# A second level of products in the second layer, shared by pairs of batches

## The chip, the cores and the metric

The kernel runs on one core of a Trainium2 chip. The metric is the device time of one execution in microseconds. The engines are named as in the profile: PE (matmuls), PEld (its weight loads), DVE (vector), ACT (scalar), POOL (GpSimd) and SP, whose queue issues nearly all DMAs.

## The reference

The input has 8 batches of 12 heads, 448 tokens and 64 columns per head, in float32. Attention with normalised q and k gives a row of 768 numbers per token, and two layers without biases follow:

```python
q_n, k_n = rmsnorm(q, g_q), rmsnorm(k, g_k)
scores = matmul(q_n, k_n.transpose(0, 1, 3, 2)) / sqrt(64)
attn = exp(scores - max) / (sum + 1e-9)
x = matmul(attn, v)              # heads side by side: (8*448, 768)
h = x @ w_in                     # w_in: (768, 2048)
out = (h - tanh(h)) @ w_out      # w_out: (2048, 768)
```

The output has 3584 rows (8 batches of 448) and 768 columns. The weights arrive as float64 and are rounded to float32 in the kernel.

## The kernel before

The order of the work on every engine is written out by hand. There are two streams. The attention stream goes through 48 steps, six per batch; a step treats two heads, and steps with `s >= 2 * NP` (12 and later) are made by `slot(s)`. The MLP stream is the generator `mlp()`, which yields after each matmul. `slot` begins with a visit (values of head pair `s` and scores of `s + 1`, on PE, then `divide`), and then has 14 points; before each, `run(...)` lets the MLP stream issue matmuls for a share of the step, and at the point a piece of attention's other work is issued: squares, sums of squares and a power on POOL (`power_blocks`, L488), `scale_blocks` (L495), transposes (L505, L509), sums of the probabilities (`add` L562, `add_third` L568, `add_last` L575), and their folding (L672 to L704). `gap_ns(s)` says how much MLP work goes into a step, and the MLP stream runs about one batch behind attention: steps 12 and later carry batches 1 to 6, and batch 7's two layers come after the last step.

Both layers use a Strassen product in the form with seven products and shared sums. The first layer (`hidden(b)`) splits the 768 columns in two halves, the 2048 in two halves, and the batch's 448 tokens in two halves of 224. It has four sets (`SETS`) of seven products, each of 2 x 3 matmuls of 128 x 128 weights with 224 moving columns. The sums of the tokens' quarters are made in `divide`, on POOL (L733 to L736), into the tile `tt`. The activations `h - tanh(h)` go into `gT` by `shrink` (L811, L812). The second layer (`project(b)`) has three sets of seven products, each of 8 matmuls of 224 columns; the sums of `gT` that it needs are made in `factors` and `rest` (L822 to L824 on DVE and POOL, L856 on POOL) into the tile `tg`. Finished output rows are transposed on DVE by `store` (L870) into one of two `th` buffers, and four DMAs (L875) per buffer write them out two products later.

The products are issued in the order `ORDER = (1, 5, 6, 2, 3, 7, 4)`. Products 2, 3 and 7 accumulate into the PSUM banks of 1, 5 and 6. There are three such banks, `mm0` to `mm2`, in turn. After each product DVE or ACT reads the bank (`use`). Work that can wait by one product is put into `late["todo"]`.

The seven combinations of each layer's weights are made once, in batch 0, and stored in DRAM (`w_in_dram`, `w_out_dram`). From batch 1 on a ring of six SBUF slots is filled from there by SP, in the order of `ring_steps`; `ring_load` is called four products ahead (L397, L399).

Of the kernel before, what the change touches and what calls it, by code (L numbers as in the profile page):

```python
# [20 lines left out]
NCH = 4  # L21
# [123 lines left out]
def bounded_path(tc, ctx, q, k, v, moe_w_in, moe_w_out, out, g_col, ident, ones, half_ones, neg_half, early):  # L145
# [32 lines left out]
    SETS = CF // 4  # L178
    ORDER = (1, 5, 6, 2, 3, 7, 4)
# [18 lines left out]
    gp = pool("gp", bufs=1)  # L198
    wp_stack = ctx.enter_context(ExitStack())
# [14 lines left out]

    def load(s, names):
        b, hp = steps[s]
        for name in names:
            src = {"q": q, "k": k, "v": v}[name]
            if s == 0 and name != "v":
                t = early[name]  # L220
            else:
                shape = [CP, 2, NCH, D] if name == "q" else [P, NCH, 2, D] if name == "k" else [P, 2, NCH, D]
                t = nat.tile(shape, F32, name=f"{name}_nat", bufs=3 if name == "v" else 2)
                fetch(nc, name, t, src[b, 2 * hp : 2 * hp + 2], in_order(s))
# [9 lines left out]
    BLOCKS = {1: 0, 2: 1, 4: 2, 7: 3, 5: 4, 6: 5, 3: 6}  # L234
    w_out_dram = scratch.tile([P, 7, HC, HF, P], F32, name="w_out")
# [140 lines left out]
    def ring_slot():  # L376
# [4 lines left out]
    ring_steps = [  # L381
        (b, layer, j, p)
        for b in range(1, B)
        for layer, count in ((0, SETS), (1, HC))
        for j in range(count)
        for p in ORDER
    ]
    ring_tiles = {}

    def ring_load(to):  # L390

        for n in range(len(ring_tiles), min(to, len(ring_steps))):
            b, layer, j, p = ring_steps[n]
            t = ring_tiles[ring_steps[n]] = ring_slot()
            if layer == 0:
                assert kept[1] > j
                nc.sync.dma_start(out=t[:, : 2 * HALF], in_=w_in_dram[j, p])  # L397
            else:
# [55 lines left out]
    def load_blocks(s):  # L454
        b, hp = steps[s]
        t = loaded["qk", s] = late["blocks"].tile([P, 2, NJ, BL], F32, name="qk_nat", bufs=2)
# [249 lines left out]
    def divide(s, av):  # L706
        b, hp = steps[s]
        rs = whole.pop(s)
        x = xT[b, hp] = xp.tile([P, S], F32, name="xT")
# [15 lines left out]
        if hp < HC:  # L725
            return
        c = hp - HC
        if c == 0:
            tt[b] = tp.tile([P, 3, HC, HS], F32, name="tt", bufs=1)
        eng = nc.vector if b == 0 and c == HC - 1 else nc.gpsimd  # L730
        x11, x12, x21, x22 = (xT[b, r][:, n : n + HS] for r in (c, hp) for n in (0, HS))
        t1, t2, t4 = (tt[b][:, i, c] for i in range(3))
        eng.tensor_tensor(out=t1, in0=x12, in1=x11, op=ALU.subtract)  # L733
        eng.tensor_tensor(out=t2, in0=x22, in1=t1, op=ALU.subtract)  # L734
        eng.tensor_tensor(out=x12, in0=x22, in1=x12, op=ALU.subtract)
        eng.tensor_tensor(out=t4, in0=x21, in1=t2, op=ALU.subtract)  # L736
# [16 lines left out]
    def products(b, layer, count, width, depth, moving, done_with):  # L753
# [8 lines left out]
        def product(j, p, bank, first):  # L762
# [21 lines left out]
            for fn in now:  # L784
                fn()

# [9 lines left out]
    def hidden(b):  # L796

        g = late["g"] = gp.tile([P, CF, S], F32, name="gT")
# [676 lines left out]
```

## Time and profile before

| | |
|---|---|
| Median of 3 runs | 1382.25 us (1381.95 to 1382.39) |
| Profiled execution | 1382.1 us, span 1380.2 us |
| Mean granted PE clock | 0.995 |
| PE busy | 1347.5 us (98%) |
| PEld busy | 1127.5 us (82%) |
| DVE busy | 891.1 us (65%) |
| ACT busy | 551.7 us (40%) |
| POOL busy | 553.7 us (40%) |
| DMA, mean | 181 GB/s |

Busy times are sums over one profiled execution. PE's matmuls overlap, so PE's busy time says that it was occupied, not that it ran at its peak. One matmul of the program leaves two records in the trace. The first 286 us hold batch 0, whose weights are still being made; after them the steps repeat, and the last 148.5 us of PE's work hold MLP matmuls alone.

### The profile page before, as it was taken

The page shows a single profiled execution, that of the slowest core. Times are in us where ns is not written, and L with a number is a line of the kernel's source. Part 1 is how long each engine was busy: PE and PEld are TensorE (multiplying, and loading weights), DVE is VectorE, ACT ScalarE, POOL GpSimd, SP SyncE. Part 2 cuts the span into 40 slices and gives each one's busy share as a digit, 9 for nine tenths or more (in the row PEclk, how much of TensorE's full clock was granted, in tenths as well). Part 3 has the DMA queues.
Part 4 walks back from the last instruction along what each step waited for, and adds up shares of the span by engine and source line. Part 5 has one row for each costly group of instructions (what it writes and reads, how often), then busy time and mean ns, then how long its engine had stood idle before and what let it go on. Part 6 is the DMA issues. An engine that isn't in the chain of part 4 may idle for free.

```text
span 1380.2 us, 29907 instructions
## 1 busy us (share of the span) xinstructions
PE 1347.5 (98%) x11840; PEld 1127.5 (82%) x11840; DVE 891.1 (65%) x1378; ACT 551.7 (40%) x1314; POOL 553.7 (40%) x345
## 2 busy tenths in 40 slices
PE   7989899999999999999999999999999999999997
PEld 3467654478998998899899889989988998999997
DVE  4999889856854776567765568547765677533311
ACT  7856555244433443334433344334433344211100
POOL 4656566224632356215542346323563155302300
PEclk9999999999999999999999999999999999999999
DMA  7789788965676567567657656765665665556664
GB/s 169 180 226 238 242 255 225 256 166 145 184 199 160 153 189 195 155 145 203 186 147 200 169 147 190 197 156 154 192 190 157 155 196 168 141 162 183 192 187 90
DMA packets 367656, 249.90 MB, mean 181 GB/s; under 512 B 281748, under 2 KB 309780, under 8 KB 367508
## 3 DMA queue, kind: packets, MB, share of 16 engines
q1 hardware_dynamic: 367504, 247.90, 66.7%
q8 instruction: 96, 1.57, 0.5%
q14 instruction: 52, 0.43, 0.1%
q10 hardware_dynamic: 4, 0.00, 0.0%
HBM read 214.40 MB, written 33.42 MB: 180 GB/s over the span
## 4 chain that ended last, share of the span: by engine, by line
PE 89%; DVE 5%; DMA 2%; SPq 2%; ACT 1%; issue 1%; POOL 0%; ACTq 0%; DVEq 0%
PE mm L775 67%; PE sc L531 8%; PE sc L597 6%; PE mm L952 5%; PE sc L585 1%; PE sc L635 1%; DVE w_out L335 1%; DVE rs L663 1%; DMA gT<-in_moe_w_in_dram 1%; DMA w_raw<-in_moe_w_in_dram 1%; DVE w_out L82 1%; SPq L125 1%; DMA w_in<-w_out 1%; DVE xT L719 0%; PE mm L635 0%
## 5 line engine op out<-in xcount | busy, mean ns | idle before, releaser
L775 PE MATMUL mm<-xT,w_f 128*128 128x224 f32 x1392 | 275.6, 354 | 0.0
L775 PEld LDWEIGHTS mm<-xT,w_f 128*128 128x128 f32 x1392 | 262.1, 190 | 10.2 <-issue 10.2
L775 PEld LDWEIGHTS mm<-gT,w_f 128*128 128x128 f32 x1344 | 252.8, 190 | 12.8 <-issue 8.4
L775 PE MATMUL mm<-gT,w_f 128*128 128x224 f32 x1344 | 263.0, 354 | 0.0
L812 POOL TENSOR_TENSOR gT<-s,th 128x448 f32<-128x448 f32 x96 | 119.9, 1256 | 329.2 <-ACT th L811 323.0
L531 PE MATMUL sc<-qT,kT 64*32 64x448 f32 (+1 forms) x3072 | 215.5, 501 | 9.3 <-ACT p_last L537 8.4
L488 POOL TENSOR_TENSOR rr_mine<-rr_mine,neg_half 128x28 f32<-128x28 f32 x33 | 158.1, 4791 | 147.6 <-DVE rr_mine L486 105.4
L775 PE MATMUL mm<-tt,w_f 128*128 128x224 f32 x1044 | 208.6, 353 | 0.0
L775 PEld LDWEIGHTS mm<-tt,w_f 128*128 128x128 f32 x1044 | 197.0, 190 | 4.4 <-issue 4.4
L775 PE MATMUL mm<-tg,w_f 128*128 128x224 f32 x1008 | 197.5, 352 | 0.0
L775 PEld LDWEIGHTS mm<-tg,w_f 128*128 128x128 f32 x1008 | 190.7, 190 | 0.0
L531 PEld LDWEIGHTS sc<-qT,kT 64*32 64x32 f32 x3072 | 70.6, 106 | 78.1 <-issue 55.1
L712 DVE TENSOR_TENSOR xT<-xT,sc 128x448 f32<-128x448 f32 x35 | 21.7, 621 | 138.6 <-PE sc L531 94.9
L597 PE MATMUL sc<-p,v_nat 64*32 64x448 f32 x1120 | 110.5, 536 | 0.0
L734 POOL TENSOR_TENSOR tt<-xT,tt 128x224 f32<-128x224 f32 x23 | 31.2, 1356 | 166.9 <-DVE xT L716 147.2
L537 ACT ACTIVATE p<-sc 128x448 f32<-128x448 f32 x132 | 71.7, 543 | 48.2 <-PE sc L531 36.3
L811 ACT ACTIVATE th<-s 128x448 f32<-128x448 f32 x96 | 54.5, 573 | 69.6 <-DVE s L841 30.2
L687 ACT COPY sum_g<-sum 32x14 f32<-32x14 f32 x280 | 56.3, 201 | 55.4 <-DVE sum L679 44.1
L952 PE MATMUL mm<-gT,w_out 128*128 128x448 f32 x192 | 74.6, 543 | 0.3 <-POOL w_out L90 0.3
L952 PEld LDWEIGHTS mm<-gT,w_out 128*128 128x128 f32 x192 | 35.7, 190 | 37.3 <-issue 34.9
L597 PEld LDWEIGHTS sc<-p,v_nat 64*32 64x32 f32 x1120 | 40.7, 107 | 29.9 <-issue 29.9
L142 POOL TENSOR_TENSOR rr<-rr,neg_half 112x8 f32<-112x8 f32 (+1 forms) x30 | 49.0, 1660 | 34.2 <-DVE rr L141 34.1
(151 smaller groups left out, 1824.0 us busy)
## 6 DMA issues: line engine op xcount, KB each, us to landing
w_f<-w_in SPq DMA_DIRECT2D x196, 384.0 KB, 3.6
w_f<-w_out SPq DMA_DIRECT2D x147, 512.0 KB, 4.5
w_raw<-in_moe_w_out_dram SPq DMA_DIRECT2D x16, 768.0 KB, 5.2
out_dram<-th SPq DMA_DIRECT2D x192, 56.0 KB, 3.6
w_in<-w_out SPq DMA_DIRECT2D x21, 384.0 KB, 5.8
qk_nat<-in_q_dram SPq DMA_DIRECT2D x132, 56.0 KB, 2.2
qk_nat<-in_k_dram SPq DMA_DIRECT2D x132, 56.0 KB, 2.3
v_nat<-in_v_dram SPq DMA_DIRECT2D x72, 96.0 KB, 4.0
```

Source lines behind the costliest of these rows:

```text
L142: nc.gpsimd.tensor_tensor(out=r, in0=r, in1=neg_half[:rows], op=ALU.pow)
L488: nc.gpsimd.tensor_tensor(out=mine, in0=mine, in1=neg_half[:, :1].to_broadcast([P, 2 * NJ]), op=ALU.pow)
L531: nc.tensor.matmul(tiles[h][i * BL : (i + 1) * BL, :n], lhsT=kT[r, c * P + at : c * P + at + BL], rhs=qT[r, first : first + n], start=True ...
L537: nc.scalar.activation(p[:, h, c if c < 2 else 0, :], tiles[h][:, :n], AF.Exp, scale=1.0 if rr is None else rr[:, 0, 2 * c + h : 2 * c + h ...
L597: nc.tensor.matmul(av[g][i * BL : (i + 1) * BL, :S], lhsT=v_nat[keys, h, c, m * BL : (m + 1) * BL], rhs=p[keys, h], start=first, stop=True ...
L687: nc.scalar.copy(out=acc[h * BL : (h + 1) * BL, g], in_=part[g * BL : (g + 1) * BL, h * NJ : (h + 1) * NJ])
L712: nc.vector.tensor_tensor(out=x, in0=x, in1=av[1][:, :S], op=ALU.add)
L734: eng.tensor_tensor(out=t2, in0=x22, in1=t1, op=ALU.subtract)
L775: nc.tensor.matmul(bank[:, f * HS : (f + 1) * HS], lhsT=w[:, c * width + f, :], rhs=moving[p](c), start=(first and f == 0 and c == 0), sto ...
L811: nc.scalar.activation(th, h, AF.Tanh, bias=0.0, scale=1.0)
L812: eng.tensor_tensor(out=g[:, rows, cols], in0=h, in1=th, op=ALU.subtract)
L952: nc.tensor.matmul(bank[:, :S], lhsT=w_out_row(f, n // HC)[:, n % HC * P : (n % HC + 1) * P], rhs=g[:, f, :], start=(f == 0), stop=(f == C ...
```

## The change

From batch 2 on, batches are taken in pairs (2, 3), (4, 5), (6, 7). The second layer of a pair is one product with two levels. The outer level has the two batches, the two halves of the 2048 columns, and the two halves of the output columns as its quarters; its seven products come in the order `OUTER = (1, 2, 3, 7, 6, 5, 4)`. Inside each outer product, two of the three blocks of 128 output columns are made by an inner level of seven products (halves of the remaining columns, and halves of the tokens), each with 4 matmuls of 224 columns. The third block is made plainly, by 8 matmuls of 448 columns.

The first `SOON = 2` outer products need only the first batch of the pair, and are issued ahead of the first layer of the second batch; the other five follow it. `outer_sum` makes the outer combinations of the activations in place, on DVE, partly between the products of the odd first layer (`beside_hidden`). `inner_sum` makes the inner combinations on POOL into four rotating `u` tiles. `combine_outer` adds the outer products up in `acc` and `acc2`, on DVE, partly by a queue `late["calm"]` that issues one entry (at the end two) per product. The second batch's activations have a tile of their own (`g2`).

The inner combinations of the second layer's weights are made in batch 1 by `inner_steps`, one small step per product: DMAs read the outer weights from DRAM, POOL makes four sums for each of seven outer products, and DMAs write the result to `inner_dram`. The ring then loads, per outer product, four tiles of inner weights and one of plain weights.

The token sums (`x_sums`, before part of `divide`) of some batches are issued one head pair later, two chunks at once. `gap_ns` gives the steps other shares of the MLP work: three steps for a first layer, two for two outer products, four for five; six matmuls are put ahead, so that each batch's work starts before the visit. The q and k rows of one step share a tile. For the paired batches a store is issued one product after its transpose rather than two.

```diff
+    PAIRED = 2
+    OUTER = (1, 2, 3, 7, 6, 5, 4)
+    SOON = 2
+    HB = HF // 2 * P
+    inner_dram = {p: scratch.tile([P, 7 * HB], F32, name=f"w_inner{p}") for p in OUTER}
...
+    ring_steps = ring_order(1, 0, SETS) + ring_order(1, 1, HC)
+    for first in range(PAIRED, B, 2):
+        for b, outer in ((first, OUTER[:SOON]), (first + 1, OUTER[SOON:])):
+            ring_steps += ring_order(b, 0, SETS)
+            ring_steps += [(first, 2, p, part) for p in outer for part in (1, 2, 3, 4, 0)]
...
+        if hp >= HC:
+            chunks = (hp - HC,)
+            if b == PAIRED or b > PAIRED and b % 2:
+                chunks = {HC: (), HC + 1: (0, 1)}.get(hp, chunks)
+            for c in chunks:
+                x_sums(b, (c,), range(4), nc.vector if b == 0 and c == HC - 1 else nc.gpsimd)
...
+    def outer_sum(which, i):
...
+        nc.vector.tensor_tensor(out=out, in0=a, in1=z, op=ALU.subtract)
+
+    def inner_sum(p, i):
...
+        u = us[p, i] = late["pair"].tile([P, KB, HS], F32, name="u", bufs=4)
+        a, z = ((x12, x11), (x22, us.get((p, 0))), (x22, x12), (x21, us.get((p, 1))))[i]
+        nc.gpsimd.tensor_tensor(out=u, in0=a, in1=z, op=ALU.subtract)
+
+    def beside_hidden(b, j, p):
+        second = b % 2
+        if j == SETS // 2 and p == 6:
+            inner_sum(3 if second else 1, 0)
+        if second and j and p in (1, 6):
+            outer_sum(p // 6, j - 1)
+
+    def project_pair(b, ks):
...
+        outer_plan = {
+            3: {1: (0, SETS - 1), 5: (1, SETS - 1)},
+            7: {1: (2, 0), 5: (2, 1), 6: (2, 2), 2: (2, 3)},
+            6: {1: (3, 0), 6: (3, 1), 3: (3, 2), 4: (3, 3)},
+        }
+        inner_plan = {5: 0, 6: 1, 7: 2, 4: 3}
+        inner_at = {6: 0, 3: 1, 7: 2, 4: 3}
...
+        for k in ks:
+            for i, q in enumerate(ORDER):
+                ring_load(step + 5 + i // 2)
+                step_out()
...
+                yield from matmuls(bank, HS, lambda c: w[:, c], moving, first)
+                flush()
...
+            bank = mm_bank()
+            yield from matmuls(bank, S, lambda i: w[:, i], [rows(p, f, 1, slice(0, S))[:, 0] for f in range(HF)], True)
+            flush()
+            late["todo"].append(lambda p=p, v=bank[:, :S]: combine_outer(p, HC - 1, v))
...
+        for b in range(PAIRED, B, 2):
+            yield from hidden(b)
+            while late["inner"] is not None:
+                inner_step()
+            yield from project_pair(b, range(SOON))
+            yield from hidden(b + 1)
+            yield from project_pair(b, range(SOON, len(OUTER)))
...
+        if s < 2 * NP + 3:
+            return (H_NS + AHEAD_NS) / 12
+        if s < 2 * NP + 7:
+            return O_NS / 16
+        n = (s - 2 * NP - 7) % (2 * NP)
+        return (H_NS / 12, OUTER_NS * SOON / 8, H_NS / 12, OUTER_NS * (len(OUTER) - SOON) / 16)[(n > 2) + (n > 4) + (n > 7)]
```

## The prediction

> **What bounds the kernel now.** I read the page's engine table first, then the chain of waits in order of time. A "step" below is one attention head pair: a visit (its score and value matmuls), then its share of the MLP's matmuls.
>
> ```profile
> PE 1347.5 (98%) x11840; PEld 1127.5 (82%) x11840; DVE 891.1 (65%) x1378; ACT 551.7 (40%) x1314; POOL 553.7 (40%) x345
> ```
>
> ```profile
> 609.32 21.38 PE mm L775 x112
> 636.13 21.39 PE mm L775 x112
> 662.95 21.39 PE mm L775 x112
> ...
> 1223.45 148.52 PE mm L775 x784
> ```
>
> Steps start their MLP matmuls every 26.81 us: 21.38 us for 56 matmuls of 224 columns (two records each), so 0.3818 us per matmul, and 5.43 us of visit. From 286 to 1372 us PE never waits. What bounds the kernel is the number of matmul columns, so a change pays if it removes columns and the other queues still keep up.
>
> Next the table by stretches, for how much room they have (columns: length, PE, PEld, DVE, ACT, POOL):
>
> ```profile
> 636.13:662.95 26.82, 26.82 (x242) 23.50 (x241) 19.58 (x29) 11.93 (x30) 10.99 (x6) 1.00 0.59 160
> 662.95:689.76 26.81, 26.81 (x241) 23.47 (x241) 23.04 (x33) 12.10 (x32) 14.98 (x9) 1.00 0.70 205
> ```
>
> Then the timeline of DVE and of POOL around one meeting of the two:
>
> ```profile
> 508.27 1.07 DVE L562 TENSOR_TENSOR rows<-p 128x896 f32<-128x896 f32 x1
> 509.44 1.85 DVE L568 TENSOR_TENSOR rows<-rows,p_full 128x896 f32<-128x896 f32 x1
> 511.21 1.55 DVE L822 TENSOR_TENSOR tg<-gT 128x448 f32<-128x448 f32 x1
> 512.87 0.63 DVE L823 TENSOR_TENSOR tg<-gT,tg 128x448 f32<-128x448 f32 x1
> ```
>
> ```profile
> 509.08 3.20 POOL L812 TENSOR_TENSOR gT<-s,th 128x448 f32<-128x448 f32 x2 [2.39 <-ACT th L811]
> ```
>
> L568 takes 1.08 us elsewhere and L822 0.62. Both stretch while POOL's L812 runs, and POOL's pair takes 3.20 us in place of 2.26. DVE operations with two SBUF operands and POOL sums take turns. Transposes, reductions and adds that read PSUM are not stretched (L672 takes 1.10 us with POOL and without). A power (L488) is no such partner:
>
> ```profile
> 625.26 4.78 POOL L488 TENSOR_TENSOR rr_mine<-rr_mine,neg_half 128x28 f32<-128x28 f32 x1 [1.71 <-DVE rr_mine L486]
> ```
>
> ```profile
> 626.68 0.55 DVE L822 TENSOR_TENSOR tg<-gT 128x448 f32<-128x448 f32 x1
> ```
>
> [...]
>
> **Part 1, fewer columns.** Two batches' second layers were 2 x 7 x 3 x 8 = 336 matmuls. Now each of seven outer products has 7 x 4 = 28 matmuls of 224 columns and 8 of 448, which count double (L952: 12.22 us for 16): 44, together 308. Saved: 28 x 3 pairs x 0.3818 = **32.1 us**. Nothing else of PE's work changes.
>
> **Part 2, prices on DVE and POOL.** From rows: a 224-wide DVE add 0.39 (L904), a 448-wide one 0.62 (L823), an 896-wide SBUF sum 1.08 (L568), a transpose 0.65 (L870), attention's DVE work 12.3 per step (its rows from L473 to L716 added). POOL: 224 wide 0.66 (L733), 448 wide 1.13 (L812 alone), so 896 wide 2.07 by that slope (an estimate). Per pair the change adds 21 combining adds, 16 outer sums (twice as wide as the 16 replaced) and 28 inner sums on POOL in place of 16 sums of half the width.
>
> **Part 3, five outer products beside attention** (two pairs, four steps each). A product is now 4 matmuls, 1.53 us, instead of 8, so a PSUM bank is wanted back in half the time. The order of instructions shows the tightest place in the second step. Its clock: visit to 5.43; 27 matmuls finish outer product 7 at 15.7; of outer product 6, inner product 1 ends at 17.3, 5 at 18.8. Inner product 6 then needs the bank of 7's third column block, which DVE frees with two adds in `combine_outer`. DVE: division to 7.3; before those adds stand, in order, instructions worth 0.39, 1.08 (scale), 0.62, 0.77, 1.23, 0.62, 0.39, 1.05, 1.08, 1.08, 1.26, 0.62, 1.10, then 1.24 for the adds themselves: 12.5, so 19.8 with no waits, 1.1 us late. POOL meanwhile has three token sums left (one needs no division and is done earlier) and three inner sums. Taking turns, DVE waits 0.7, 0.7, 0.7, 1.7 and 2.1 us before the scale, the first combining add, the second, and the two 896-wide sums: the bank is free at about 25.3, a stall of **6.5 us**. The same walk gives 1.2 us in the first step (the last inner sum of the outer product comes after the token sums: 13.5 against 12.3), 2.9 in the third (same bank, 16.9 against 14.6, and 0.6 later), 1.1 in the fourth. Together 11.7 per section, 23.4 for two; ends 1.1 (no turns taken) and 16 per section.
>
> **Part 4, two outer products** (three pairs). In their first step eight token sums stand on POOL ahead of the inner sum that product 4 wants at 12.3. Five need no division and run during the visit; three follow at 7.3 and take turns with two DVE operations of 1.08 and 1.05; then 2.07: 14.3. Loss 2.0 each, **6.0**; ends 0 and 3 each. The six matmuls put ahead of the visit hide the other start-up sums.
>
> **Part 5, the end.** The last five outer products run without attention. Starting without a visit to hide the inner sum costs 1.0. After the last matmul the old kernel needed 8.2 us (1372.0 to 1380.2). Now the last batches' stores crowd together: nine transposes write two buffers, and each buffer is held for its 0.65, four issues of 0.54 and the landing:
>
> ```profile
> out_dram<-th SPq DMA_DIRECT2D x192, 56.0 KB, 3.6
> ```
>
> about 6 us, so the ninth transpose ends some 7.6 us after the last matmul, where the old one ended after 1.1. Cost **6.0**; ends 1 and 8.
>
> **Part 6, making the inner weights** in batch 1. POOL gets 28 sums of 512 columns (about 1.27 each by the slope), SP 49 DMAs of 20.2 MB behind waits for POOL, with the ring loads queued after them. Over 165 us that is 122 GB/s more beside 172. A window of the trace (172 to 176 us) moved 416 GB/s, and ring tiles are issued four products ahead, so I take **2 us**; ends 0 and 10. Outer sums beside the odd first layer load DVE to about 22 of 26.8, less than the 23.04 that cost nothing above: 0, and about 2 per step if that cover fails. Ring traffic per pair falls from 22.0 to 16.5 MB: 0. Shared q/k tiles: the q load now waits for the transposes that the k load behind it waited for anyway: 0.
>
> **Sum** against the profiled execution's 1382.1 us (the runs' median is 1382.25): 1382.1 - 32.1 + 23.4 + 6.0 + 1.0 + 6.0 + 2.0 = **1388.4**.
>
> **Rivals.**
> The cover holds, on the other side. One mechanism: DVE frees the banks in time because POOL's sums fall into its waits for PE. For it: the step with DVE at 23.04 of 26.81 lost nothing. Against: that step had 8-matmul products and no inner sums. It decides where the third column block's bank is free before 18.8 us into the second step; altogether the kernel is faster as soon as stalls and end cost under 32 us. Price: only 1.1 x 2, start and end remain: 1382.1 - 32.1 + 2.2 + 7 = 1359; with half the turns 1371. Chance 0.38.
> Gain and loss meet within 0.2% (about 2.8 us, what a measurement of this kernel can tell from no change): 0.12.
> Transfers saturate in batch 1: PE waits for ring tiles queued behind copies; 10 more, about 1398 to 1408. Against: 416 GB/s was reached. Chance 0.08.
> The matmuls do not fall: the instruction order shows 28 and 8 per outer product, so 0.02 (it would then be slower by parts 3 to 6).
> The forecast itself, 0.40; its own range 1385 to 1402.
>
> Faster by over 0.2%: 0.38 (the cover). Slower: 0.40 + 0.08 + 0.02 = 0.50. The range 1361 to 1408 leaves out the ends of both sides.
>
> **What would show it.** PE's chain should have gaps of 5 to 7 us in the second of the five-product steps, released by DVE in `combine_outer`, and of about 2 us released by POOL's inner sum; DVE near 90% busy in those steps, with 896-wide sums stretched to 2 to 3 us; about 14 us after the last matmul. If mlp stretches there run at 0.382 us per matmul without gaps, part 3 is wrong and the time is near 1360. Gaps between 290 and 460 us released by a DMA would show part 6 wrong.

## The result and the profile after

The changed kernel takes 1421.88 us (median of 4 runs, 1421.42 to 1425.57) against 1382.16 us for the kernel before (4 runs, 1381.95 to 1382.39). The ratio is 1.0297, with a 95% interval of 1.0281 to 1.0313. The prediction was 1388.4 us with a range of 1361 to 1408: slower was right, but the kernel lost 39.7 us where 6.3 were foretold. The profiled execution took 1421.4 us (span 1419.6).

The page of the changed kernel answers the engine row of before:

```profile
PE 1337.1 (94%) x11336; PEld 1042.5 (73%) x11336; DVE 1000.0 (70%) x1459; ACT 553.1 (39%) x1326; POOL 740.6 (52%) x409
```

The 504 records fewer are 252 matmuls: 84 are the saved work of part 1, and 168 more are gone because one matmul of 448 columns stands in place of two of 224. But PE's busy time fell by 10.4 us only, and its share fell from 98% to 94%. The table of what PE waited for names the holes (columns: total us, times, longest):

```profile
PE mm L1056 <- issue: 18.5, 6, 5.1
PE mm L1056 <- POOL u L1017: 11.6, 5, 4.4
PE mm L809 <- DMA w_f<-w_in: 5.0, 4, 2.3
PE mm L809 <- DVE s L1063: 4.8, 2, 2.6
PE mm L1056 <- DVE acc L1063: 3.8, 5, 1.4
```

L1056 is the second layer's matmul, L809 the first layer's, L1017 `inner_sum`, L1063 the adds of `combine_outer` and of the products. In the kernel before, PE had no gap of over 0.15 us between 290 us and its last matmul; now gaps of over 0.15 us add up to 45.8 us there. "Issue" means that the profile shows no releaser; at the longest of these gaps, at 719 us, DVE's own list gives one. Here are DVE's and then POOL's instructions in the second of the four steps with five outer products:

```profile
713.67 2.66 DVE L584 TENSOR_TENSOR rows<-p 128x896 f32<-128x896 f32 x1
716.44 2.78 DVE L590 TENSOR_TENSOR rows<-rows,p_full 128x896 f32<-128x896 f32 x1
...
723.00 1.11 DVE L1063 TENSOR_TENSOR acc<-acc,mm 128x448 f32<-128x448 f32 x2
```

```profile
710.87 2.10 POOL L1017 TENSOR_TENSOR u<-g,u 128x896 f32<-128x896 f32 x1
712.92 2.47 POOL L1017 TENSOR_TENSOR u<-g 128x896 f32<-128x896 f32 x1
715.34 2.93 POOL L1017 TENSOR_TENSOR u<-g,u 128x896 f32<-128x896 f32 x1
```

The two 896-wide sums of attention take 2.66 and 2.78 us in place of 1.08, because POOL's inner sums stand in between. The two adds that free the bank of product 7's third block come at 723.00, and PE, which had stopped at 719.11, goes on at 724.21. That is the place and the mechanism of the prediction's part 3: 5.10 us, and 6.5 foretold. PE's own list shows the gap, and what PE does before and behind it:

```profile
717.43 1.68 PE L1056 MATMUL mm<-u,w_f 128*128 128x224 f32 x8
724.21 3.33 PE L1056 MATMUL mm<-u,w_f 128*128 128x224 f32 x8 [5.10 <-issue]
```

8 records (4 matmuls) take 1.68 us ahead of the gap and 3.33 behind it.

What the prediction lacks stands in the next view, the windows of 1 us around the same gap (columns: length, then busy PE, PEld, DVE, ACT and POOL with the number of records that touch the window, then granted PE clock, DMA share, GB/s):

```profile
722.00:723.00 1.00, 0.00 (x0) 0.00 (x0) 1.00 (x3) 0.00 (x0) 0.00 (x0) 0.98 0.09 33
723.00:724.00 1.00, 0.00 (x0) 0.00 (x0) 1.00 (x3) 0.00 (x0) 0.00 (x0) 0.50 0.00 0
724.00:725.00 1.00, 0.79 (x2) 0.78 (x3) 1.00 (x3) 0.00 (x0) 0.00 (x0) 0.50 0.00 0
...
730.00:731.00 1.00, 1.00 (x7) 1.00 (x6) 0.00 (x0) 0.72 (x2) 1.00 (x1) 1.00 0.00 0
```

PE comes back at half its clock, and keeps it until 729.8. The trace's clock record has six such stretches after 290 us and before the last matmul, of 3.41 or 6.83 us, 30.7 us together; the kernel before had none there. 25.4 us of them lie outside the gaps, and at half speed these lose 12.7 us (an estimate from the trace: half of 25.4).

### The profile page after: what moved, and what is told of

Same layout as the page of the kernel before. It is cut to its first block, busy times and chain, and to the rows that moved or that the text cites. A ratio compares the mean times of both kernels' runs of the same rounds, so it can differ in the third digit from the quotient of the medians.

```text
span 1419.6 us, 29139 instructions
## 1 busy us (share of the span) xinstructions
PE 1337.1 (94%) x11336; PEld 1042.5 (73%) x11336; DVE 1000.0 (70%) x1459; ACT 553.1 (39%) x1326; POOL 740.6 (52%) x409
## 5 line engine op out<-in xcount | busy, mean ns | idle before, releaser
L809 PE MATMUL mm<-xT,w_f 128*128 128x224 f32 x1296 | 267.9, 355 | 8.3 <-DVE s L1063 4.8
L809 PEld LDWEIGHTS mm<-xT,w_f 128*128 128x128 f32 x1296 | 244.7, 191 | 21.5 <-issue 9.5
L809 PE MATMUL mm<-tt,w_f 128*128 128x224 f32 x1044 | 208.0, 353 | 2.3 <-DMA w_f<-w_in 2.3
L809 PEld LDWEIGHTS mm<-tt,w_f 128*128 128x128 f32 x1044 | 197.0, 190 | 7.0 <-issue 3.7
L1056 PE MATMUL mm<-u,w_f 128*128 128x224 f32 x672 | 146.8, 369 | 33.3 <-issue 18.5
L1056 PEld LDWEIGHTS mm<-u,w_f 128*128 128x128 f32 x672 | 130.1, 197 | 45.2 <-issue 30.8
L857 POOL TENSOR_TENSOR gT<-s,th 128x448 f32<-128x448 f32 x60 | 80.1, 1341 | 148.0 <-ACT th L856 104.3
L1056 PE MATMUL mm<-gT,w_f 128*128 128x224 f32 (+1 forms) x480 | 133.9, 432 | 0.0
L737 DVE TENSOR_TENSOR xT<-xT,sc 128x448 f32<-128x448 f32 x32 | 19.8, 619 | 154.4 <-PE sc L553 77.9
L1056 PEld LDWEIGHTS mm<-gT,w_f 128*128 128x128 f32 x480 | 91.7, 192 | 36.6 <-issue 36.1
L857 POOL TENSOR_TENSOR g<-s,th 128x448 f32<-128x448 f32 x36 | 46.3, 1292 | 129.3 <-ACT th L856 105.4
L709 ACT COPY sum_g<-sum 32x14 f32<-32x14 f32 x280 | 56.3, 201 | 144.0 <-DVE sum L701 122.1
L1056 PE MATMUL mm<-g,w_f 128*128 128x224 f32 (+1 forms) x360 | 101.7, 436 | 0.7 <-DVE acc L1063 0.7
L1056 PEld LDWEIGHTS mm<-g,w_f 128*128 128x128 f32 x360 | 69.8, 196 | 30.5 <-issue 28.6
L770 POOL TENSOR_TENSOR tt<-xT,tt 128x224 f32<-128x224 f32 x46 | 43.5, 946 | 55.1 <-DVE xT L741 33.2
```

The lines of the kernel that those rows point to most:

```text
L709: nc.scalar.copy(out=acc[h * BL : (h + 1) * BL, g], in_=part[g * BL : (g + 1) * BL, h * NJ : (h + 1) * NJ])
L737: nc.vector.tensor_tensor(out=x, in0=x, in1=av[1][:, :S], op=ALU.add)
L770: eng.tensor_tensor(out=out, in0=a, in1=z, op=ALU.subtract)
L809: nc.tensor.matmul(bank[:, f * HS : (f + 1) * HS], lhsT=w[:, c * width + f, :], rhs=moving[p](c), start=(first and f == 0 and c == 0), sto ...
L857: eng.tensor_tensor(out=g[:, rows, cols], in0=h, in1=th, op=ALU.subtract)
L1056: nc.tensor.matmul(bank[:, :n], lhsT=w(i), rhs=mv, start=(first and i == 0), stop=(i == len(moving) - 1), skip_group_check=not first,)
```

## The experiments

Single executions are compared where no interval is given. The kernel before ran between 1379.6 and 1383.6 us over all of them, so a difference of under some 4 us between two single runs says little by itself; there the gaps in the trace decide. A "section" is the four steps with five outer products, measured from the last value matmuls (`p_last`) of one visit to those of another; without waits it would take 55 matmul units of 0.3818 us and a visit of 5.43 us per step, 105.7 us. In the changed kernel the two sections took 125.5 and 127.7.

**e1, e2, e3: which of the added sums makes the waits.** In e1 the inner sums on POOL are cut to 2 of 224 columns, in e2 each is replaced by a power on 11 numbers that takes as long, in e3 the outer sums on DVE are cut to 2 of 224 columns.

```diff
-        nc.gpsimd.tensor_tensor(out=u, in0=a, in1=z, op=ALU.subtract)
+ e1:    nc.gpsimd.tensor_tensor(out=u[:, :, :2], in0=a[:, :, :2], in1=z[:, :, :2], op=ALU.subtract)
+ e2:    nc.gpsimd.tensor_tensor(out=u[:, 0, :11], in0=ones[:, :11], in1=z[:, 0, :11], op=ALU.pow)
-        nc.vector.tensor_tensor(out=out, in0=a, in1=z, op=ALU.subtract)
+ e3:    nc.vector.tensor_tensor(out=out[:, :, :2], in0=a[:, :, :2], in1=z[:, :, :2], op=ALU.subtract)
```

e1 was expected so:

> Leaves out nearly all of the inner sums on POOL (2 of 224 columns are computed, all waits stay), so the rows of the paired second layers are not the real ones. Theory A (POOL's sums and DVE's two-operand work take turns on SBUF, both queues run late, PE loses 46 us in gaps and about 15 us more because gaps of 4 to 5 us are followed by half clock): gaps before L1056 that POOL released (4.4 us twice, 1.9 us) go, the gaps of 5.1 us in the second steps fall to about 1, those in the first steps from 4.8 together to under 1, the half-clock stretches go; the gaps at the stores (2.2 and 2.6 us before the next first layer) and the 3.6 us of ring waits in batch 1 stay. Time about 1375, DVE's 448-wide pair L597 back to 1.26 us. Rival B (DVE has too many instructions whatever POOL does): only the POOL-released gaps go, about 1405. Rival C (ring and stores): under 5 us gained, 1417 to 1422.

Measured 1376.78 us: gaps 14.4 us in place of 45.8, sections 112.0 and 113.7, one half-clock stretch after 290 us. So the inner sums cost 45 us, with the gaps and the half clock that they bring. Without them a section is still 6.3 and 8.0 us above its 105.7.

e2:

> Replaces each inner sum on POOL by a power of 11 elements, which keeps POOL for about 2.1 us by the slope of the powers of 8 and 28 elements, but is not seen to hold up DVE; the rows of the paired second layers are not the real ones. Theory A (taking turns): DVE's rows near it are no longer stretched, the second steps' gap of 5.1 us falls to 1 to 2 and its half clock goes, the POOL-released gaps fall from 4.4 to about 3; time about 1390. Rival B1 (POOL's queue time alone): all gaps stay, 1418 to 1422. Rival B (DVE's own load): little change, 1415 to 1422.

Measured 1399.22 us, halfway. In the second step the three powers and attention's two sums now stand like this:

```profile
711.27 2.11 POOL L1018 TENSOR_TENSOR u<-ones,u 128x11 f32<-128x11 f32 x1
713.35 2.90 POOL L1018 TENSOR_TENSOR u<-ones,g 128x11 f32<-128x11 f32 x1
...
713.20 1.07 DVE L584 TENSOR_TENSOR rows<-p 128x896 f32<-128x896 f32 x1
714.38 1.09 DVE L590 TENSOR_TENSOR rows<-rows,p_full 128x896 f32<-128x896 f32 x1
```

POOL is as busy as before, but DVE's sums take 1.07 and 1.09 us, and the gap falls from 5.1 to 0.94 us. So the taking of turns makes that gap. The gaps released by POOL in the first steps stay or grow (4.2 and 4.2 us with two products, from 4.4 and 4.4; 2.5 and 2.5 with five, from 0.4 and 0.4): those are POOL's queue. Taken this way, about 22.4 us of the inner sums' 45 are queue time and about 22.7 are turns, each with the half clock behind its gaps.

e3:

> Leaves out nearly all of the outer sums on DVE (2 of 224 columns are computed, all waits stay): the rows of the paired second layers are not the real ones. Some 17 us of DVE work per pair go. Theory A: what is late at the 5.1 us gap is the queue between the division and the adds of the third column block, in which no outer sum stands, so that gap stays within 1 us; gaps in the first steps shrink from 4.8 to about 2; time 1408 to 1416. Rival B (DVE's total load): the gaps shrink with the load, about 1395 or below.

Measured 1416.49 us: both 5.1 us gaps are where they were. The outer sums are not the cause of these gaps, and less DVE work alone gains 5 us. All gaps fell from 45.8 to 41.1 us, but the half clock outside the gaps rose from 25.4 to 33.4 us, which took back some 4 us.

**e4: the bank freed by ACT.** ACT copies the third block out of its bank and DVE adds from SBUF.

```diff
+            if third:
+                y, v = early["sq"].rearrange("p a d -> p (a d)")[:, :S], y
+                nc.scalar.copy(out=y, in_=v)
```

> Same result as the changed kernel. The third column block is copied out of its bank by ACT, and DVE adds it from SBUF, so that bank no longer waits for DVE. Theory A (DVE's queue as a whole is late): the 5.1 us gap moves to the next bank that DVE must free, inner product 3, and shrinks only by what PE does in between, about 3 us, which also spares the half clock: 1408 to 1416. Rival D (this one bank is the fault): both gaps of 5.1 us, those of 1.6 us and their half clock go, and no other appears: about 1400.

Measured 1432.06 us. The 5.1 us gap becomes 2.7, but in the third step DVE is now late by 4.2 us where nothing above 1.6 us stood. The gap shrank as theory A had it, but the wait moved on to the third step, with more two-operand SBUF work on DVE, and the time missed both theories. The gaps of e4 add up to 45.7 us, as many as in the changed kernel; what rose is the half clock outside them, from 25.4 to 43.8 us. Half of that, 9.2 us, is nearly the whole loss of 10.2. Some of it is the position of a gap alone: the 2.55 us gap in the first section's first step was followed by half clock here and not in the changed kernel.

**e5: the clock by itself.** The kernel before, with waits of known length and nothing added to DVE or POOL.

```diff
+                    for i in range(PLAN[b, j]):          # 2 to 12 copies on ACT
+                        dst = spare[:, i % 2 * HS : (i % 2 + 1) * HS]
+                        nc.scalar.copy(out=dst, in_=src)
+                        src = dst
...
+                nc.tensor.matmul(bank[:, :HS], lhsT=ident, rhs=waste[1], start=True, stop=True)
```

> The kernel before (1382 us, no gap over 0.3 us after 290 us), with 24 waits put into it: after the first product of each set of batches 2 to 7's first layers, a chain of 2 to 12 copies of 224 columns on ACT, and one more matmul that reads the last copy and must run before the next product. Nothing is added to DVE or POOL. Each gap should be about 0.6 us plus 0.42 us per copy, 1.4 to 5.7 us, together some 85 us, and the 24 matmuls 9 us. Theory A (an idle stretch of PE is itself followed by PE at half its granted clock): half-clock stretches after the gaps from some length on, 2.5 to 4.4 us by the changed kernel's gaps (2.2 us had none, 2.5 us had one in some places, 4.4 us always); with one stretch of 3.4 or 6.8 us for each of 12 to 16 gaps, 20 to 55 us lost beyond the gaps: 1496 to 1530. Theory B (the half clock came from the crowd on DVE and POOL, not from PE's idleness): no half clock beyond that of the kernel before, 1470 to 1480.

Measured 1537.28 us. The gaps were 1.28 to 8.04 us, 101.3 us together; with 9.2 us for the 24 matmuls, 44.7 of the 155.2 us added are neither, and the clock record has 109.2 us at half clock. 79.4 us of these lie outside the gaps and lose 39.7, so the half clock explains all but 5.0 of the 44.7. All 17 gaps from 2.9 us on were followed by half clock, none of the three up to 1.69 us, and two of four between 2.0 and 2.5 us. The windows behind three gaps, first one of 2.91 us that began at 1196.9, then one of 2.03 us (1090.6), last one of 2.51 us (1010.3):

```profile
1200.00:1202.00 2.00, 2.00 (x6) 1.80 (x7) 0.00 (x0) 0.00 (x0) 0.00 (x0) 0.50 0.64 106
1202.00:1204.00 2.00, 2.00 (x10) 1.88 (x9) 0.00 (x0) 0.00 (x0) 0.00 (x0) 0.74 0.80 121
...
1092.00:1094.00 2.00, 1.42 (x7) 1.42 (x8) 1.90 (x3) 0.50 (x2) 1.38 (x2) 0.96 0.84 307
1094.00:1096.00 2.00, 2.00 (x7) 1.82 (x6) 1.22 (x2) 0.67 (x4) 2.00 (x2) 0.50 0.70 269
...
1013.00:1015.00 2.00, 2.00 (x12) 2.00 (x12) 0.00 (x0) 0.00 (x0) 0.00 (x0) 1.00 0.69 111
```

A gap of 2.03 us cost half clock and one of 2.51 us did not. A fixed grid fits this: the starts of the half-clock stretches after 290 us lie whole multiples of 3.41 us apart, 50, 49, 43, 8 and 20 of them in the changed kernel and 31 between the two starts in the rows above (1093.84 and 1199.64 us). With intervals of 3.41 us that end at these starts, the gaps of e5 that were not followed by half clock left PE idle for at most 1.69 us of one interval, those that were followed for at least 2.03 us. The gap of 2.03 us lies in one interval, the one of 2.51 us is cut into 1.61 and 0.90 us. In the changed kernel it was at most 1.89 and at least 2.22 us: of its two gaps of 2.55 us at one place of the two sections, the first (694.09 us) had 1.56 us in one interval and was not followed, the second (1034.76 us) had 2.22 us and was. The second interval of the gap at 719.11 kept the half clock with 1.25 us of idleness, so the limit is not one number; why is open. A gap of 3.33 us was not followed either (e1, at 328.5 us).

**e6: matmuls in the gaps.** Matmuls that nobody needs stand ahead of the products that wait longest, so that PE is not idle there.

```diff
+                n = {(1, 4): {2: 10, 4: 10, 6: 4}[b], (7, 6): 5, (6, 6): 12}.get((p, q), 0) if b < 6 or p == 1 else 0
+                for i in range(n):
+                    nc.tensor.matmul(spare[:, :HS], lhsT=w[:, 0], rhs=rows(p, 0, 1, low)[:, 0], ...)
```

> The changed kernel, with matmuls of 224 columns into an unused bank put ahead of the products that wait longest: 12 ahead of inner product 6 of outer product 6 (two places, 5.1 us gaps), 10, 10 and 4 ahead of product 4 of the first outer product of each pair (4.4, 4.4 and 1.9 us), and 5 ahead of inner product 6 of outer product 7 (two places, 2.6 us). They compute nothing that is used and fit into gaps that are there anyway. Theory A (idle gaps lead to half clock, 15.4 us in the changed kernel): gaps after 290 us fall from 46 to about 20 us, the half-clock stretches after those places go, and the time falls by 10 to 15 us to 1407 to 1412. Theory B (the clock falls for another reason, or the added matmuls take time themselves): 1420 to 1430.

Measured 1418.69 us, between the two. At the filled places the half clock did go, and the two-product first steps fell from 28.6 and 29.5 to 26.9 us. But a section took 128.7 and 129.7 us. In the second step:

```profile
716.25 4.70 PE L1124 MATMUL sc<-g,w_f 128*128 128x224 f32 x24
721.63 1.75 PE L1056 MATMUL mm<-u,w_f 128*128 128x224 f32 x8 [0.68 <-DVE acc L1063]
```

PE then ran on at full clock and met the same late DVE at 744.1 us, with a gap of 4.02 us in place of 1.56, and at 786.2 with 3.14 in place of 2.17, each followed by half clock again. At 744.1 DVE's second 896-wide sum had been stretched to 2.95 us, where it took 1.08 in the changed kernel. In a section, therefore, the half clock is not a term that can be taken off alone: DVE and POOL are behind, and a PE that is slower only waits less at the next place.

**e7, e8: two orders.** In e7 the token sums of batches 3 and later are issued at the first point behind the division, so that an inner sum goes ahead of them. In e8 attention's sums of probabilities are issued four points later in the second step, behind the adds that free the bank.

```diff
+ e7:           if b > PAIRED:
+                   late["x"].append(lambda c=c: x_sums(b, (c,), range(4), nc.gpsimd))
+ e8:       work[3], work[4], work[6] = work[3][1:], [], work[6][1:]
+           work[7] = [(True, lambda: add(s + 1, False))]
+           work[8] = [(True, lambda: add_third(s + 1))]
```

> The changed kernel, with one part moved: the token sums on POOL of batches 3 and later are issued at the first point of attention's other work behind the division, not in the division. So the inner sum that product 4 of the first outer product waits for stands ahead of them on POOL. Theory A (POOL's order makes the 4.4 us gaps in the first steps of the two outer products): these gaps fall under 1.5 us in the pairs (2, 3) and (4, 5) and their half-clock stretches go, 6 to 7 us of gaps and 5 us of clock; the first of the five-product steps may gain 1 to 2 us as well: 1406 to 1412. Rival C (POOL and DVE only take turns, so that order does not matter): 1418 to 1424.

e7 measured 1415.52 us. The two-product first steps fell from 28.6 and 29.5 to 25.5 us (22.2 without waits) and their half clock went; the first of the five-product steps rose from 32.7 and 34.2 to 37.3 and 37.1, since an inner sum that now stands ahead of the token sums runs beside the division. In the first section the division's two sums (L741) took 4.58 us in place of 3.16, and the step's longest gap rose from 2.55 us without half clock to 3.85 us with 6.83 us of it. Right for the place it was meant for, wrong for the sum.

> The changed kernel; in the second of the four steps with five outer products (two places in the kernel) attention's sums of probabilities and what hangs on them (two 896-wide sums, the last sums, the folding) are issued four points later, behind the adds that free the bank of outer product 7's third block. The work is the same. Theory A (the 5.1 us gap is the taking of turns between these two 896-wide sums and POOL's three inner sums, which stand ahead of those adds on DVE): the gap falls from 5.1 to under 1.5 us, DVE's two sums take about 1.1 us each in place of 2.7, and the half-clock stretch behind it goes: 7 to 8.5 us at each of two places, 1405 to 1409. Rival D (DVE has too much work in the step in whatever order): the wait comes back later in the step or at the next division, 1417 to 1424.

e8 measured 1415.92 us. The second step fell from 34.5 to 29.0 and from 34.1 to 30.3 us, but the first section's third step rose from 28.5 to 33.8; in the second section it stayed at 28.6. A section took 125.3 and 124.0 us. Rival D is nearer in the time, but the wait came back in one of the two sections only.

**e9 to e12: more room for the section.** e9 gives the odd first layer three and a half steps and the five products three and a half, with the token sums at the seventh point. On top of e9, e10 adds a third store buffer and spreads the making of the inner weights; on top of e10, e11 frees the third block's bank at once, and e12 makes one inner sum of four on DVE.

```diff
+ e9:  return ((H_NS / 12,) * 3 + (OUTER_NS * SOON / 8,) * 2 + (odd,) * 3 + ((odd + five) / 2,) + (five,) * 3)[n]
+ e10: if b and b <= PAIRED and (layer or late["turn"] % 3): inner_step()
+ e11: combine_outer(p, HC - 1, bank[:, :S])
+ e12: eng = nc.vector if i == 2 else nc.gpsimd
```

> The changed kernel with the odd first layer given three and a half steps in place of three, and the five outer products behind it three and a half in place of four (so a stretch of the five products carries an eighth less of attention's work); the token sums of batches 3 and later are issued at the seventh point of the step, the first two chunks together. The work is the same. Theory A (in the five-product steps DVE's and POOL's SBUF work, which take turns, do not fit beside 21 us of matmuls; a wait mended in one place comes back in the next): the waits of a section fall by about the half step's work that leaves it, 6 to 8 us for each of two sections, and the two-product steps gain 6 us as with the token sums late: 1396 to 1404. Rival D (only the order inside the steps matters): no more than the token sums' gain, 1413 to 1418.

> e9_shares, with two more parts: every third store of the paired batches uses a third buffer, and in batch 1 the steps that make the inner weights are issued after two of every three products of the first layer rather than after each, which spreads their transfers. Theory A: the wait behind the store transposes (2.2 us in the fourth of the five-product steps) and the waits for ring tiles in batch 1 (2.3 and 1.3 us) go, and the end needs 1 to 3 us less: 4 to 7 us under e9_shares. If a transfer that lands later only moves these waits: within 2 us of e9_shares.

> e10_shares_stores, and the adds (or the copy) that free the bank of an outer product's third block are issued directly behind its matmuls, not behind the next product's. If the order on DVE and ACT ahead of these adds makes the waits that are left: 2 to 6 us under e10_shares_stores. If DVE has no room (theory A), or waits for PE in these adds with attention's work queued behind: within 2 us, or slower.

> e10_shares_stores, with one of the four inner sums of each outer product made on DVE (about 1.1 us) in place of POOL (2.07 us). If the time in which one engine holds up the other decides, this shortens it by 1 us in each product: 2 to 6 us under e10_shares_stores. If DVE's own busy time decides: 3 to 8 us slower, since each five-product section gives DVE five more sums, 5.5 us.

Measured 1410.12, 1416.44, 1414.02 and 1419.35 us. e9 gained less than theory A said and more than rival D: the odd first layer and the section that follows it take 204.6 and 204.5 us together, where the changed kernel took 207.5 and 209.3. e10 lost in batch 1: gaps of 3.9 and 2.6 us there and 2.1 us in the next first layer, against 2.3 and 1.3 us in the changed kernel; its third store buffer took the wait behind the stores away in the first section (1.3 us) and shortened it in the second (1.2 to 0.8). e11 (2.4 us under e10) and e12 (2.9 over it) are within what single runs can tell; by their steps, the mixed step and the three five-product steps of e12 took 133.5 and 133.4 us against 130.3 and 131.8 in e10, so DVE's added time weighed no less than the turns it saved.

**e13, e14, e15: the second level out of the sections.** The outer products beside attention are made plainly, three blocks of 8 matmuls of 448 columns. e13 does so for all five, e14 is e13 with the token sums at the seventh point and the third store buffer, e15 is e14 with products 5 and 4 on two levels again.

```diff
+    def plain(b, p):
+        return b < B - 2 and p in (3, 7, 6, 5, 4)
...
+            for m in range(HC):
+                w = ring_tiles[b, 2, p, 5 + m].rearrange("p (f d) -> p f d", d=P)
+                bank = mm_bank()
+                moving = [rows(p, f, 1, slice(0, S))[:, 0] for f in range(HF)]
+                for i, took in enumerate(matmuls(bank, S, lambda i: w[:, i], moving, True)):
...
+                late["todo"].append(lambda m=m, v=bank[:, :S]: combine_outer(p, m, v))
```

> The changed kernel, but the five outer products that run beside attention (pairs (2, 3) and (4, 5)) are made without the second level: three blocks of 8 matmuls of 448 columns each, 48 units of 0.3818 us in place of 44, no inner sums on POOL and no inner adds on DVE. The pairing of batches, its outer sums and the adds in acc stay, and so does the second level elsewhere. A section has 5 x 4 x 0.3818 = 7.6 us more matmuls. Theory A (the second level's sums beside attention make the waits): a section takes 113.4 us plus 0 to 3, in place of 125.5 and 127.7, its half clock goes, and the time is 1392 to 1399. Rival E (the pairing itself makes them): waits of over 2 us and half clock stay in these steps, and the time is 1415 to 1430.

Measured 1390.24 us. A section takes 113.2 us, which is what its columns and visits add up to (240 x 0.3818 + 4 x 5.43 = 113.4), with no wait of over 0.3 us and no half clock. The four steps, each from the end of one visit to the end of the next, first of the changed kernel, then of e13 (columns as in the table above; the steps begin within 0.3 us of the marks that the sections are measured by):

```profile
671.47:704.38 32.91, 28.16 (x246) 20.29 (x237) 26.43 (x31) 10.77 (x30) 30.99 (x15) 1.00 0.45 126
704.38:738.85 34.47, 29.37 (x230) 22.23 (x222) 27.98 (x37) 9.43 (x27) 21.87 (x10) 0.90 0.38 98
738.85:767.40 28.55, 26.99 (x221) 18.14 (x213) 19.11 (x30) 9.28 (x27) 21.52 (x11) 1.00 0.46 127
767.40:797.20 29.80, 26.92 (x217) 19.08 (x209) 21.59 (x39) 9.20 (x27) 3.60 (x1) 1.00 0.65 125
```

```profile
672.32:700.99 28.67, 28.67 (x211) 14.05 (x203) 15.25 (x21) 10.71 (x28) 10.59 (x7) 1.00 0.32 81
700.99:729.13 28.14, 28.14 (x199) 13.65 (x191) 21.90 (x31) 8.65 (x25) 8.87 (x5) 1.00 0.37 101
729.13:757.30 28.17, 28.17 (x199) 13.68 (x190) 16.41 (x26) 8.68 (x25) 7.58 (x4) 1.00 0.42 95
757.30:785.50 28.20, 28.20 (x206) 14.83 (x198) 18.56 (x30) 9.29 (x26) 4.78 (x1) 1.00 0.66 125
```

PE is busy in the whole of each of e13's steps. DVE's 95.1 us and POOL's 78.0 fall to 72.1 and 31.8. The pairing of batches with its outer sums and stores costs these steps nothing; the second level does, for 7.6 us of matmuls saved. Not all of that is POOL's work: e1, which keeps the second level but leaves out nearly all of the inner sums, took 112.0 and 113.7 us for a section, about as long as the plain blocks. 2.3 and 3.4 us of that are the wait behind the stores in its fourth step; the rest was not told apart.

> e13_plain_five with the token sums of batches 3 and later at the seventh point of the step and a third store buffer. If these parts add up as they did apart (6 us for the two-product steps, 1 to 2 us for the end): 1385 to 1392. If the token sums only move their wait: 1392 to 1399.

Measured 1383.45 us: the mended parts added up, to a little more than foretold. 4.4 us per pair of waits stayed in the two-product steps.

> e14_plain_five_mended, with the second level again in the last two (5 and 4) of the five outer products, so 8 inner sums on POOL in a section in place of 0 or 20. It saves 2 x 4 x 0.3818 = 3.05 us of matmuls per section. If so little of it fits into the free time of POOL and DVE: 4 to 6 us under e14_plain_five_mended. If inner sums cost in proportion to their number (20 of them cost 13 to 20 us per section): 5 to 10 us over it.

Measured 1388.98 us, as the second answer foretold: the two sections take 114.6 and 113.9 us, with 6.1 us less matmuls in both together, and the step behind each is 1.7 and 1.6 us longer, of which 0.99 and 0.93 are a wait of the even first layer for a ring tile. Two of five products on two levels gain nothing.

**e16, e17: what is left of the second level.** In the two-product steps of the pairs (2, 3) and (4, 5), e16 makes product 1 plainly too, e17 both; the rest is e14. The last pair keeps two levels.

```diff
+ e16:   return b < B - 2 and p in (1, 3, 7, 6, 5, 4)
+ e17:   return b < B - 2 and p in (1, 2, 3, 7, 6, 5, 4)
```

> e14_plain_five_mended (1383.45 us) with product 1 of the pairs (2, 3) and (4, 5) made plainly too, so that of their products only product 2 has the second level; its four inner sums are made during product 1's blocks. It adds 4 x 0.3818 = 1.5 us of matmuls per pair and should take away the 3.9 and 0.5 us of waits in the two-product steps: 2 to 3 us per pair, 1377 to 1380. If the inner sums' turns with DVE make a wait there all the same: 1382 to 1386.

> e16_second_only with product 2 of these pairs plain as well, so the second level is left for the last pair alone, where seven products save 7 x 4 x 0.3818 = 10.7 us. Against e16: 1.5 us more matmuls for each of two pairs, 3 us slower if product 2's inner sums were hidden there, level or faster if they were not. Against the kernel before: 10.7 us less for matmuls, some 4 to 5 us for making the inner weights in batch 1 and 2 us for a later end: 1376 to 1383.

e16 takes 1377.82 us (7 runs, 1375.94 to 1378.42) against 1381.21 for the kernel before on that chip (19 runs): ratio 0.9972, interval 0.9961 to 0.9983. e17 takes 1381.64, ratio 0.9998, interval 0.9990 to 1.0007. So product 2's inner sums, made during product 1's plain blocks, are hidden: the two two-product steps take 46.1 us, 47.3 in e17. e16's page:

```profile
PE 1338.6 (97%) x11048; PEld 981.8 (71%) x11048; DVE 942.1 (68%) x1387; ACT 549.6 (40%) x1310; POOL 624.5 (45%) x361
```

Its gaps after 290 us are 3.7 us together, 2.3 of them in batch 1.

## Why the prediction was wrong

By its own steps, with lengths of steps measured as the sections are:

- *Part 1, columns:* right. e13's waitless sections show the price per unit too.
- *Part 3, the sections.* The walk through DVE's and POOL's queues was right in kind and nearly in size as far as gaps go: 14.2 and 14.0 us of gaps per section against 11.7 (second step 5.1 for 6.5, third 1.6 for 2.9, fourth 2.8 and 2.6 for 1.1, first 4.8 for 1.2). Its terms for the second step add up to 25.7 rather than 25.3 us, which changes little. In the first step 2.55 of the 4.8 us come from a wait that the walk did not have: the 1.26 us `add_last` was stretched to 3.62 behind two whole inner sums, and ACT's copy that frees the third block's bank stands behind copies (L709) that wait for what DVE does next (a line of DVE's list, then one of ACT's):

```profile
688.28 3.62 DVE L597 TENSOR_TENSOR rows<-rows,p_last 64x448 f32<-64x448 f32 x2
...
696.01 0.53 ACT L1070 COPY acc<-mm 128x448 f32<-128x448 f32 x1
```

  But the sections lost 19.8 and 21.9 us, 41.7 in place of 23.4. The largest part of the difference is a term that the sum does not have at all: PE at half clock after the gaps, 16.8 us of it outside them, which lose 8.4 us in the two sections and 12.7 in the whole kernel. The kernel before shows it, a 5.43 us gap at 162.4 us and 6.83 us of clock 0.5 from 164.3 us on, and the prediction did not read that row (first PE's list, then the windows):

```profile
167.80 1.74 PE L531 MATMUL sc<-qT,kT 64*32 64x448 f32 x14 [5.43 <-ACT p_last L537]
...
168.00:170.00 2.00, 2.00 (x15) 0.52 (x6) 0.40 (x1) 0.47 (x2) 0.93 (x1) 0.50 0.97 332
```

  That it was costed at nothing is the step that failed first. Another 5 us came in the steps beside the sections, which the prediction had at nothing too.
- *Part 4, two outer products:* mis-sized, and the second step that failed. 4.4, 4.4 and 1.9 us of gaps in place of 2.0 each, and half clock behind the first two; their steps lost 6.4 and 7.3 us. The walk's terms add up to 13.5 rather than the 14.3 us that it gives (7.3, three sums of 0.66, 1.08, 1.05, 2.07), so by them the loss was 1.2 each. It let five token sums run during the visit. POOL's list shows why they did not:

```profile
538.08 1.14 POOL L857 TENSOR_TENSOR gT<-s,th 128x448 f32<-128x448 f32 x1
539.18 2.09 POOL L1017 TENSOR_TENSOR u<-gT 128x896 f32<-128x896 f32 x1
541.24 1.04 POOL L770 TENSOR_TENSOR tt<-xT 128x224 f32<-128x224 f32 x1
...
549.50 2.06 POOL L1017 TENSOR_TENSOR u<-gT,u 128x896 f32<-128x896 f32 x1
```

  Two inner sums and the last set's activations kept POOL until 541.2, and the eight token sums then took 8.3 us, since three of them took 1.4 or 1.5 us and two 0.9 or 1.0, not 0.66. The page of the kernel before had such a price, beside the row of 0.66 (L733) that the walk took for all of them; the second of its four token sums took 1.36 us in the mean:

```profile
L734 POOL TENSOR_TENSOR tt<-xT,tt 128x224 f32<-128x224 f32 x23 | 31.2, 1356 | 166.9 <-DVE xT L716 147.2
```

- *Part 5:* nearly right. 13.0 us after the last matmul (14 foretold, 8.2 before): transposes wait for their buffer's store to land, 1.83 and 0.87 us for the last two. The last transpose ended 5.0 us after the last matmul (7.6 foretold). The last five products had one gap, of 0.25 us, not 1.0.
- *Part 6:* mis-sized, 4.8 us in batch 1 in place of 2. The sign that was named for it came: gaps of 2.29 and 1.27 us at 328.5 and 337.9 us that a ring tile's DMA released.
- *The sum:* -32.1 + 41.7 + 5.5 (beside the sections) + 15.5 (two products, the third pair's 1.9 with them) + 4.8 (end) + 4.8 (batch 1) + 0.2 = 40.4; measured in the profiled execution 39.3. Against the forecast the kernel lost 33.0 us more: 13.4 are gaps (45.8 in place of the 32.4 us of stalls in the sum), 12.7 half clock, and 8.1 are in neither; the end took 1.2 less.
- *Powers and sums:* that a power is no partner in the taking of turns was right. e2's powers took 2.1 to 2.9 us, and DVE's two-operand sums beside them took 1.07 and 1.09 us; beside the changed kernel's inner sums of 2.47 and 2.93 us they took 2.66 and 2.78.
- *The rivals:* the cover did not hold, and its point of decision was rightly placed: PE wanted the third block's bank 18.9 us into the second step (18.8 foretold; 719.1, the visit from 700.2), and DVE freed it at 23.9 (foretold 25.3). DVE was 67 to 81% busy in the four steps, not near 90%. Transfers did not saturate beyond part 6.

What stays open: 45.8 us of gaps, 12.7 of half clock and 4.8 of end, less the 32.1 saved, make 31.2 us; the other 8.1 of the 39.3 lie in shorter gaps or in slower stretches. Some 3 us of them are in three visits at the sections' ends, which took 6.8 to 7.0 us in place of 5.43, gaps of 0.4 to 0.6 us included; the rest was not told apart. How much of the half clock a section would keep if DVE were in time cannot be separated, as e6 shows.

## What to carry to other kernels

A gap on PE can cost more than its length. In the changed kernel six of nine gaps of over 2 us were followed by half speed for 3.41 or 6.83 us; the limit lay between 1.69 and 2.03 us of idleness in one interval of 3.41 us in e5, and between 1.89 and 2.22 in the changed kernel. So a wait of over 2 us goes into the sum with up to 1.7 or 3.4 us more (half of 3.41 and 6.83, an estimate), and which gap gets it depends on where it falls. In the first three steps of the changed kernel's first section DVE was busy for 19.1 to 28.0 us and POOL, which takes turns with it, for 21.5 to 31.0, of 28.6 to 34.5; a wait that was mended at one bank there came back at the next (e4, e6, and e8 in one of two sections). Take work out, which gained 31.6 us (e13), rather than move it, which lost 10.2 (e4) or gained 3.2 and 6.0 (e6, e8). Before a level is added that saves columns, set its saving per product (1.53 us) against the sums it needs (four on POOL, of 2.1 to 2.9 us here), and use it only where these are hidden (e16).

## What was not expected of the hardware

- The starts of the half-clock stretches stand on a fixed grid of 3.41 us; in e5 a gap of 2.03 us that lay in one interval of that grid halved the clock, and one of 2.51 us that the grid cuts into 1.61 and 0.90 us did not.
- In e5 the half clock, where it came, lasted 3.41 or 6.83 us after gaps of 2 to 7 us; the three gaps of 7.3 to 8.0 us had 10.24 us, part of it inside the gap.
- POOL's busy time by itself did not stretch DVE: beside powers of 2.11 and 2.90 us (e2) DVE's two 896-wide sums took 1.07 and 1.09 us, beside 896-wide sums of 2.47 and 2.93 us (the changed kernel) 2.66 and 2.78.
